# An attention kernel's output projection, by seven block products in place of eight

## The chip, the cores and the metric

The kernel runs on one core of a Trainium2 chip. The metric is the time of one execution on the device in microseconds (us). The kernel before was run three times; a further execution was taken by the hardware profiler, and every profile line below comes from that one.

The engines are named as the profile names them: PE is TensorE's matmuls and PEld its weight loads, DVE is VectorE, ACT is ScalarE, POOL is GpSimd, SP is SyncE, which here only issues transfers. SPq marks rows of SP's queue. L423 is line 423 of the kernel.

## The reference

Sixteen tiles of 128 rows make up x (2048 x 512, bf16). A gate branch B runs beside attention A, and the result is x + A(xn) * silu(B(xn)):

```
xn = layernorm(x)
q  = (xn @ wq) as 32 heads of 128          # k, v: caches, 2048 keys, 32 heads
p  = softmax(q k^T * 128**-0.5)
s  = concat over heads of (p v) @ wo       # wo: 4096 x 512
h  = gelu(layernorm(xn) @ w1), shifted by rows in four column groups
x1 = xn + h @ w2
g  = silu(x1 + gelu(layernorm(x1) @ w3) @ w4)
out = x + s * g
```

## The kernel before

**Units and slots.** The 32 heads are done in eight groups of four (g = 0 to 7; the change's groups two to seven are g = 1 to 6). A unit is one head with one query tile of 512 rows; there are 128, ordered by group, then query tile (qt = 0 to 3), then head (hh = 0 to 3). A unit has eight slots of 256 keys. The main loop (L921 and on) runs over slots n = 8u + p and records every engine's instructions in program order; no scheduler moves them later. In each slot `s_slot` issues two score matmuls of 512 columns into one of two score buffers (`ps_s`) and one exponential of 128x1024 on ScalarE (L423), whose output `pT` is kept for the PV matmuls. These come ten slots later (`pv_slot`, two of 512 columns). The scores of a slot can start only when the exponential two slots earlier has read its buffer.

**Queries.** From unit 16 to 125 the queries of two heads are made together by seven products of 256 columns in place of eight (`product`, `q_take`, `q_part`), in slots 0, 2, 5, 8, 9, 12 and 13 of every sixteen. ScalarE evicts 128x256 twice for it (`q_take`, L393, slots 0 and 5); VectorE does four sums (`q_part`, L400 to L407).

**Softmax sums.** VectorE adds a unit's exponentials up (`add_first` L429, `add_next` L434, `fold` L438, `fold_last` L442). SP transposes the result by a transfer (`turn`, L467, into `tT`); VectorE reduces it (L472) five slots later, takes the reciprocal (L478), and two more transfers through DRAM spread it to all partitions (`dr`, then `rb`). In slot 7 `norm` (L496) multiplies a unit's PV result by it and writes its part of `oT` (128 x 4 heads x 512 rows, two buffers). Its columns come out in an order that the turn gives (row 4r + j next to row j), and the projection picks them with a step of four (`o_cols`).

**Output projection.** Once the four heads of a query tile are normed, `wo_todo` gets its four row tiles t. For each, `wo_mm` accumulates four matmuls of 512 columns (one head each: weights are `oT` columns, the moving operand is `wo_h`) in one PSUM bank (`ps_wo`, tag "xm", one buffer), one row tile per unit, in slots 1, 3, 4 and 6 of even units and 0, 2, 3 and 6 of odd ones (`at_wo`, L965). `wo_post` then adds the bank to `sacc[t]` (fp32, SBUF) on VectorE (L560), in slot 7.

**Gate and end.** `xall` holds the gate tiles. For the query tiles of LATE (2 and 3), `y_scale` and `y_add` multiply `sacc` by the gate and add x before the last groups (L526, L531), and groups 6 and 7 gate their part first (L553) and add it. For the others the last `wo_post` does it (L569 to L572). The last units go another way (from L995 on).

**Queues.** Every transfer of the kernel in attention is issued by SP. GpSimd issues none and is idle from the first 100 us on.

Of the kernel before, what the change touches and what calls it, by code (L numbers as in the profile page):

```python
# [17 lines left out]
def kernel(  # L18
# [25 lines left out]
    NT = Sq // P  # L44
    QT = Sq // 512
# [5 lines left out]
    HG = 4  # L51
# [20 lines left out]
    xall = const.tile([P, NT, D], BF16, name="xall")  # L72
# [21 lines left out]
    drp = ent(pool("drp", 4, bass.MemoryType.DRAM))  # L94
    psO = ent(pool("psO", 2, PSUM))
# [28 lines left out]
    XS = 3 * QT + 1  # L124
    units = [(g, qt, hh) for g in range(NG) for qt in range(QT) for hh in range(HG)]
    LATE = (QT - 2, QT - 1)
    GY = NG - 2
# [61 lines left out]
    xn2T = {}  # L189
    w4_sb = [pR.tile([P, D], BF16, name=f"w4_sb{i}") for i in range(FC)]  # L190
    h2 = {}

# [30 lines left out]
    def ln1_norm(t):  # L223
        if t == 1:
            pin(nc.vector.tensor_scalar(
                out=xall[:, t, :], in0=xin.pop(t)[:], scalar1=less[:], scalar2=rs1[:, t:t + 1],
                op0=ALU.add, op1=ALU.mult))
            return
        src = xin.pop(t)[:]
        w = D // 2 if t == 0 else D  # L230
        for c in range(0, D, w):
            norm_to(xall[:, t, :], src, mv1, rs1, t, slice(c, c + w))

    def tr_pe(t):
        tp = psO.tile([P, DC, P], FP32, tag="ps_o", name="ps_o")
        for dc in range(DC):
            mm(tp[:, dc, :], xall[:, t, dc * P:(dc + 1) * P], ident[:], True, True)
        pin(nc.scalar.activation(out=xnT[:, :, t * P:(t + 1) * P], in_=tp[:], func=ACT.Identity))

    def tr_pe_split(t, parts=((0, 2), (2, 4))):  # L240
        for i in range(2):
            tp = psO.tile([P, 2, P], FP32, tag="ps_o", name="ps_o")
            for j in range(2):
                dc = 2 * i + j
                mm(tp[:, j, :], xall[:, t, dc * P:(dc + 1) * P], ident[:], True, True)
# [6 lines left out]
    def tr_dma(t):  # L252
        pin(nc.sync.dma_start_transpose(out=xnT[:, :, t * P:(t + 1) * P], in_=xall[:, t, :]))
# [21 lines left out]
    def x1(t, ps):  # L275
        pin(nc.vector.tensor_tensor(out=xall[:, t, :], in0=ps[:], in1=xall[:, t, :], op=ALU.add))

    def ln2(t):
# [4 lines left out]
        norm_to(y[:], xall[:, t, :], mv2, rs2, t)  # L283
# [17 lines left out]
    def x2(t, ps):  # L301
        pin(nc.vector.tensor_tensor(out=xall[:, t, :], in0=ps[:], in1=xall[:, t, :], op=ALU.add))

    def gate_tanh(t):
        th = token(False, "th")
        pin(nc.scalar.activation(out=th[:], in_=xall[:, t, :], func=ACT.Tanh, scale=0.5))
        return th

    def gate_silu(t, th):
        pin(nc.vector.scalar_tensor_tensor(  # L310
            out=xall[:, t, :], in0=th[:], scalar=1.0, in1=xall[:, t, :], op0=ALU.add, op1=ALU.mult))
# [11 lines left out]
    def q_copy(u, eng=None):  # L323
        pl, tag = (pR, "qR") if u < HEAD else (qtp, "qT")
        qT = pl.tile([P, 512], BF16, tag=tag, **(dict(bufs=HEAD) if u < HEAD else {}), name="qT")
        if eng is None:
            pin(nc.vector.tensor_copy(out=qT[:], in_=st[u].pop("psq")[:]))
        else:
            pin(nc.scalar.activation(out=qT[:], in_=st[u].pop("psq")[:], func=ACT.Identity))
        st[u]["qT"] = qT  # L330
# [51 lines left out]

    def q_take(v, i):
# [768 lines left out]
```

## Time and profile before

| | us |
|---|---|
| runs, median of 3 (lowest, highest) | 1236.2 (1235.44, 1236.68) |
| the profiled execution | 1236.51 |
| its span, first to last instruction | 1234.7 |
| PE busy | 1228.3 |
| ACT busy | 1105.8 |
| DVE busy | 1030.3 |
| POOL busy | 26.7 |

The page gives for each group of instructions its line, engine, operation and tiles (output <- inputs), the shapes, the count, the busy time and mean duration of one in ns, and the idle time before them with what ended it. The time-ordered view gives the start in us, the duration in us of all instructions merged into the row (xN of them), engine, line, operation and tiles; a bracket at the end is the idle time ahead of it and what ended that. Instructions of one engine overlap in their records, so that a row's duration is not the distance to the next: that is read from the starts or ends of successive rows. Busy shares are unions of such records.

### The profile page before, as it was taken

Reading aid. Unit: us, or ns where it says so; the run is one execution under the profiler, and the core shown is the slowest. Engines: PE = TensorE matmul, PEld = TensorE weight load, DVE = VectorE, ACT = ScalarE, POOL = GpSimd, SP = SyncE. Lnnn points to the kernel's source line nnn. Section 1 sums busy time; section 2 is a strip of 40 time slices with the busy share of each in tenths; the row PEclk is TensorE's granted clock in tenths of the full one; section 3 lists DMA queues with packets and bytes.
Section 4 is the critical chain, followed back from the end, with each engine's and each line's share of the span. In section 5 each row is a group of like instructions: output and inputs, shape, how many; then the busy total and the mean of one; then the engine's idle time right before and its main releaser. Section 6 shows DMA issues by size and latency. Waiting matters only on the chain.

```text
span 1234.7 us, 17537 instructions
## 1 busy us (share of the span) xinstructions
PE 1228.3 (99%) x6267; PEld 644.5 (52%) x6267; DVE 1030.3 (83%) x1647; ACT 1105.8 (90%) x1237; POOL 26.7 (2%) x75
## 2 busy tenths in 40 slices
PE   9999999999999999999999999999999999999998
PEld 6444444455555555555555555555555555555555
DVE  7712778899888888988889888888889999999997
ACT  6345998899999999999999999999999999999996
POOL 5300000000000000000000000000000000000000
PEclk9999999999999999999999999999999999999999
DMA  7761122564344433454244523553346535553342
GB/s 176 171 139 32 29 41 65 95 99 94 57 85 99 104 60 81 88 111 81 62 86 100 111 50 76 102 103 75 74 86 108 105 63 86 103 104 69 77 80 67
DMA packets 244056, 107.75 MB, mean 87 GB/s; under 512 B 194816, under 2 KB 227712, under 8 KB 243968
## 3 DMA queue, kind: packets, MB, share of 16 engines
q1 hardware_dynamic: 243408, 106.17, 42.8%
q8 instruction: 49, 0.80, 0.3%
q14 instruction: 39, 0.32, 0.1%
q10 hardware_dynamic: 560, 0.46, 0.1%
HBM read 67.50 MB, written 2.36 MB: 57 GB/s over the span
## 4 chain that ended last, share of the span: by engine, by line
PE 94%; DVE 3%; DMA 2%; ACT 1%; issue 0%; POOL 0%; DVEq 0%; ACTq 0%
PE ps_s L112 39%; PE ps_o L112 37%; PE ps_wo L112 8%; PE ps_q L112 8%; PE ps_m L112 2%; DVE acc L434 1%; DMA tT<-acc 1%; ACT pT L423 1%; DMA rb<-dr 0%; DVE sm L472 0%; DVE oT L496 0%; DMA xin<-in_A_x_dram 0%; DMA dr<-rc 0%; PE ps_oh L112 0%; DVE acc L438 0%
## 5 line engine op out<-in xcount | busy, mean ns | idle before, releaser
L423 ACT ACTIVATE pT<-ps_s 128x1024 bf16<-128x1024 f32 x1016 | 1016.3, 1025 | 56.6 <-PE ps_s L112 25.9
L112 PE MATMUL ps_s<-qT,kT 128*128 128x512 bf16 (+1 forms) x2064 | 609.1, 377 | 0.0
L112 PE MATMUL ps_o<-pT,vb 128*128 128x512 bf16 x1984 | 589.9, 379 | 0.0
L434 DVE TENSOR_TENSOR acc<-acc,pT 128x2048 bf16<-128x2048 bf16 x254 | 306.9, 1208 | 55.1 <-ACT pT L423 54.7
L112 PEld LDWEIGHTS <-kT 128*128 128x128 bf16 x2064 | 232.6, 113 | 143.9 <-issue 1.0
L112 PEld LDWEIGHTS <-vb 128*128 128x128 bf16 x1984 | 194.0, 98 | 216.8
L429 DVE TENSOR_TENSOR acc<-pT 128x2048 bf16<-128x2048 bf16 x127 | 155.4, 1223 | 37.7 <-ACT pT L423 35.1
L112 PE MATMUL ps_wo<-wo_h,oT 128*128 128x512 bf16 x496 | 186.2, 379 | 0.0
L438 DVE TENSOR_TENSOR acc<-acc 128x1024 bf16<-128x1024 bf16 x127 | 87.4, 688 | 2.5
L496 DVE TENSOR_TENSOR oT<-ps_o,rb 128x512 bf16<-128x512 f32 x127 | 86.6, 682 | 2.4 <-DMA rb<-dr 2.0
L112 PEld LDWEIGHTS <-oT 128*128 128x128 bf16 x528 | 59.0, 112 | 52.5 <-issue 0.7
L472 DVE TENSOR_REDUCE sm<-tT 128x4 f32<-128x512 bf16 x124 | 83.9, 677 | 2.2 <-DMA tT<-acc 2.0
L112 PEld LDWEIGHTS <-wc 128*128 128x128 bf16 x440 | 43.1, 98 | 53.8 <-issue 2.6
L560 DVE TENSOR_TENSOR sacc<-ps_wo,sacc 128x512 f32<-128x512 f32 x96 | 65.7, 684 | 0.0
L112 PEld LDWEIGHTS <-wq_h 128*128 128x128 bf16 x398 | 38.9, 98 | 46.3
L112 PE MATMUL ps_q<-xnT,wq_h 128*128 128x256 bf16 (+1 forms) x288 | 61.1, 298 | 0.4 <-DVE sacc L548 0.4
L407 DVE TENSOR_TENSOR qT<-ps_q,tq 128x512 bf16<-128x512 f32 x55 | 38.0, 691 | 22.8 <-PE ps_q L112 22.3
L442 DVE TENSOR_TENSOR acc<-acc 128x512 bf16<-128x512 bf16 x127 | 52.9, 417 | 0.5
L293 ACT ACTIVATE h2T<-ps_s 128x1024 bf16<-128x1024 f32 x28 | 28.6, 1023 | 25.9 <-PE ps_s L112 25.9
L112 PEld LDWEIGHTS <-w_sb 128*128 128x128 bf16 x368 | 33.5, 98 | 29.6
L112 PE MATMUL ps_s<-xn2T,w_sb 128*128 128x512 bf16 x224 | 48.8, 379 | 0.0
L112 PE MATMUL ps_q<-xs,wc 128*128 128x256 bf16 x246 | 47.0, 273 | 0.0
(102 smaller groups left out, 586.7 us busy)
## 6 DMA issues: line engine op xcount, KB each, us to landing
rb<-dr SPq DMA_DIRECT2D x127, 256.0 KB, 4.1
vb<-in_A_v_cache_dram SPq DMA_DIRECT2D x62, 256.0 KB, 3.1
wq_h<-in_A_wq_dram SPq DMA_DIRECT2D x32, 128.0 KB, 3.1
wo_h<-in_A_wo_dram SPq DMA_DIRECT2D x32, 128.0 KB, 2.9
w_sb<-in_B_w_dram SPq DMA_DIRECT2D x8, 256.0 KB, 5.0
kT<-in_A_k_cache_dram SPq DMA_TRANSPOSE x128, 2.9
xl<-in_A_x_dram SPq DMA_DIRECT2D x16, 128.0 KB, 3.2
dr<-rc SPq DMA_DIRECT2D x127, 2.0 KB, 1.5
```

Of the source, the lines that this page charges most:

```text
L112: pin(nc.tensor.matmul(out=out, lhsT=lhsT, rhs=rhs, start=start, stop=stop, **kw))
L293: pin(nc.scalar.activation(out=h2[c, f][:], in_=ps[:], func=ACT.Gelu_apprx_tanh))
L407: pin(nc.vector.tensor_tensor(out=s["q"][:, 1:3, :], in0=ps[:], in1=s["u"][:].unsqueeze(1).to_broadcast([P, 2, 256]), op=ALU.add))
L423: pin(nc.scalar.activation(out=s["pT"][-1][:, jj:jj + 2, :], in_=sps[:], func=ACT.Exp, scale=SCALE))
L429: pin(nc.vector.tensor_tensor(out=s["acc"][:], in0=s["pT"][0][:], in1=s["pT"][1][:], op=ALU.add))
L434: pin(nc.vector.tensor_tensor(out=a[:], in0=a[:], in1=st[u]["pT"][i][:], op=ALU.add))
L438: pin(nc.vector.tensor_tensor(out=a[:, 0:2, :], in0=a[:, 0:2, :], in1=a[:, 2:4, :], op=ALU.add))
L442: pin(nc.vector.tensor_tensor(out=a[:, 0, :], in0=a[:, 0, :], in1=a[:, 1, :], op=ALU.add))
L472: pin(nc.vector.tensor_reduce(out=sm[:], in_=s["tT"][:], axis=mybir.AxisListType.X, op=ALU.add))
L496: pin(nc.vector.tensor_tensor(out=to, in0=o, in1=rb, op=ALU.mult))
L560: pin(nc.vector.tensor_tensor(out=sa, in0=ps[:], in1=sa, op=ALU.add))
```

## The change

For groups 1 to 6 (`BLOCK`) the product of `oT` and `wo` is done on 2 x 2 blocks, by seven products in place of eight. The rows of a query tile are halved into two column halves of `oT` (WL, WR: row tiles 0 and 1, and 2 and 3), the inner dimension into head pairs (UP, DOWN), the columns of `wo` into halves of 256. i = 0, 1 names the tile in each half, so a product for one i serves the row tiles i and i + 2, and one (g, qt, i) is a block of sixteen slots. `wo_sum` makes four sums of weight blocks per group, `o_sum` four sums of `oT` blocks per query tile, on VectorE. `wo_product` issues two matmuls of 256 columns for each of the seven products.

Of the five sums that products go into, three are taken by VectorE from PSUM into `sacc` (`wo_take`: 512 columns in slot 13, 256 columns in slot 21, which is slot 5 of the next sixteen). Two are evicted by ScalarE to SBUF (`wo_aside`, fp32, slots 7 and 15, two staging buffers) and added into DRAM (`both`) by transfers that GpSimd issues; group 6's `wo_join` adds them into `sacc` by four more transfers per block.

`sacc` becomes a tile for two row tiles, in column halves. The query columns are turned where queries are evicted (`q_copy`, `q_take`, `q_part` read PSUM with a step of four), so `oT` comes out in row order and is read without a step; the score matmuls then read the paired queries in runs of 64. `xall` is split: tiles 0 to 7 (`xlo`) live only until attention starts, their gates are stored to DRAM by GpSimd (`gate_silu`) and loaded again for group 7 (`fin_load`). `y_add` is gone; `y_scale` lets a transfer add x. Group 6's own gating leaves `wo_post`.

```
+    AWAY = NT // 2
...
+    TW = (2, 1, 0, 1)
...
+        if t < AWAY:
+            gates[t] = keep.tile([P, D], BF16, tag=f"gate{t}", name="gate")
+            pin(nc.gpsimd.dma_start(out=gates[t][:], in_=xg(t)))
...
+        if u in TURN:
+            src = src.rearrange("d (r j) -> d j r", j=4)
+            dst = dst.rearrange("d (j r) -> d j r", j=4)
...
+            for j in range(2):
+                x = q[:, 2 * j:2 * j + 2]
+                st[v + j] = dict(qT=x.rearrange("d h j r -> d j h r"))
+            out = q[:, 0]
+        pin(nc.scalar.activation(out=out, in_=turned(v, s["ps"][:])[:, 0], func=ACT.Identity))
...
+    def wo_sum(g, i):
+        w = wog[g]
+        b11, b12, b21, b22 = (w[:, k, c] for k in (UP, DOWN) for c in (WL, WR))
+        out = b12 if i == 2 else pS.tile([P, 2, D // 2], BF16, tag=f"tw{i}", bufs=TW[i], name="tw")[:]
+        a, b = ((b12, b11), (b22, tw.get((g, 0))), (b22, b12), (b21, tw.get((g, 1))))[i]
+        pin(nc.vector.tensor_tensor(out=out, in0=a, in1=b, op=ALU.subtract))
...
+    def o_sum(g, qt, i):
+        o = oTs[(g, qt)]
+        a11, a12, a21, a22 = (o[:, k, c] for c in (WL, WR) for k in (UP, DOWN))
+        out = pS.tile([P, 2, D // 2], BF16, tag=f"so{i}", bufs=1, name="so")
+        a, b, op = ((a21, a22, ALU.add), (so.get(0), a11, ALU.subtract),
+                    (a11, a21, ALU.subtract), (a12, so.get(1), ALU.subtract))[i]
+        pin(nc.vector.tensor_tensor(out=out[:], in0=a, in1=b, op=op))
...
+    def wo_product(g, qt, i, k):
+        if k == 1:
+            wo_ps[0] = psX.tile([P, 2, D // 2], FP32, tag="xm", name="ps_wo")
...
+        side, a, b = {
+            1: (0, a11, b11),
+            2: (0, a12, b21),
+            3: (1, so.get(3), b22),
+            4: (1, a22, tw.get((g, 3))),
+            5: (1, so.get(0), tw.get((g, 0))),
+            6: (0, so.get(1), tw.get((g, 1))),
+            7: (1, so.get(2), tw.get((g, 2))),
+        }[k]
+        for j in range(2):
+            mm(wo_ps[0][:, side, :], a[:, j, i * P:(i + 1) * P], b[:, j, :],
+               k in (1, 6) and j == 0, True, skip_group_check=True)
+
+    def wo_aside(g, qt, i):
+        stage = pS.tile([P, 2, D // 2], FP32, tag="tm", bufs=2, name="stage")
+        pin(nc.scalar.activation(out=stage[:], in_=wo_ps[0][:], func=ACT.Identity))
+        kw = dict(accum_op=ALU.add)
+        if (qt, i) not in shared:
+            shared[qt, i] = keep.tile([P, 2, D // 2], FP32, tag=f"both{qt}{i}", name="both")
+            kw = {}
+        pin(nc.gpsimd.dma_start(out=shared[qt, i][:], in_=stage[:], **kw))
+
+    def wo_take(g, qt, i, last):
+        sa, ps = sp[qt, i], wo_ps[0]
+        cols = slice(2, 3) if last else slice(0, 2)
+        pin(nc.vector.tensor_tensor(
+            out=sa[:, cols], in0=ps[:, 1:2] if last else ps[:], in1=sa[:, cols], op=ALU.add))
+
+    def wo_join(qt, i):
+        sa, both = sp[qt, i], shared.pop((qt, i))
+        for j in (1, 2, 3):
+            pin(nc.gpsimd.dma_start(out=sa[:, j], in_=both[:, 0], accum_op=ALU.add))
+        pin(nc.gpsimd.dma_start(out=sa[:, 3], in_=both[:, 1], accum_op=ALU.add))
...
-        if (g * QT + qt) * HG + hh in TURN:
-            return o.rearrange("k (p j) -> k j p", j=4)[:, ts, :]
...
+        pin(nc.gpsimd.dma_start(out=sacc[t], in_=halves(xsrc[t]), accum_op=ALU.add))
-
-    def y_add(t):
-        xl = fin.pop(t)
-        pin(nc.vector.tensor_tensor(out=sacc[t][:], in0=sacc[t][:], in1=xl[:], op=ALU.add))
...
+    for g in BLOCK:
+        for qt in range(QT):
+            u0 = ((g * QT + qt) * HG + 6) * SPU
+            if qt == 0:
+                for i, n in ((0, -19), (2, -11), (1, -1), (3, 3)):
+                    o_at(u0 + n, wo_sum, g, i)
+            for i, n in ((2, 5), (0, 7), (1, 11), (3, 15)):
+                o_at(u0 + n, o_sum, g, qt, i)
+            for i in range(2):
+                a = u0 + 16 * i
+                for k, n in ((1, 6), (7, 7), (2, 10), (4, 11), (6, 14), (5, 15), (3, 17)):
+                    steps[a + n].append((wo_product, g, qt, i, k))
+                for n in (7, 15):
+                    steps[a + n].append((wo_aside, g, qt, i))
+                o_at(a + 13, wo_take, g, qt, i, False)
+                o_at(a + (21 if g < BLOCK[-1] or qt < QT - 1 or i == 0 else 18), wo_take, g, qt, i, True)
+                if g == BLOCK[-1]:
+                    o_at(a + 22, wo_join, qt, i)
+                    if qt in LATE:
+                        for j in range(2):
+                            at(a + 42 + 5 * j, lambda t=4 * qt + i + 2 * j: y_scale(t))
...
         run_steps(n, product)
+        run_steps(n, wo_product)
+        run_steps(n, wo_aside)
         run_steps(n, q_take)
...
+        if u // HG == (NG - 1) * QT + 1 and u % HG in (2, 3):
+            at_wo = ([4, 5, 6, 7], [2, 3, 5, 6, 7])[u % 2]
```

155 lines of the change are left out of this document (90 added, 65 removed).

## The prediction

> **What bounds the kernel now.** First the page's busy shares and its chain of waits, then the busy time by stretches.
>
> ```profile
> PE 1228.3 (99%) x6267; PEld 644.5 (52%) x6267; DVE 1030.3 (83%) x1647; ACT 1105.8 (90%) x1237; POOL 26.7 (2%) x75
> PE 94%; DVE 3%; DMA 2%; ACT 1%; issue 0%; POOL 0%; DVEq 0%; ACTq 0%
> 100.00:150.00 50.00, 50.00 (x233) 23.50 (x232) 24.02 (x32) 37.58 (x41) 0.00 (x0) 1.00 0.07 11
> 550.00:650.00 100.00, 100.00 (x505) 52.76 (x504) 85.62 (x131) 95.70 (x107) 0.00 (x0) 1.00 0.40 82
> ```
>
> In a stretch the columns are sum, PE, PEld, DVE, ACT, POOL, granted clock, share of the DMA engines, GB/s. Through attention TensorE never rests, at full clock. ScalarE is next at 95.7%, so whatever it gets in addition has to be followed place by place. The time-ordered view of one pair of units shows the rhythm:
>
> ```profile
> 69.81 12.25 PE L112 MATMUL ps_o<-w_sb,h2T 128*128 128x512 bf16 x56
> ...
> 605.36 0.59 PE L112 MATMUL ps_s<-qT,kT 128*128 128x512 bf16 x2
> 605.79 0.59 PE L112 MATMUL ps_o<-pT,vb 128*128 128x512 bf16 x2
> 606.22 0.38 PE L112 MATMUL ps_q<-xnT,wq_h 128*128 128x256 bf16 x2
> 606.44 0.59 PE L112 MATMUL ps_s<-qT,kT 128*128 128x512 bf16 x2
> ...
> 615.08 0.59 PE L112 MATMUL ps_s<-qT,kT 128*128 128x512 bf16 x2
> ```
>
> The 56 matmuls of the first row follow each other at (12.25 - 0.38)/55 = 0.2158 us. A slot is two score and two PV matmuls, 4 x 0.2158 = 0.863 us, plus what is put behind them: here a pair of 256-column query products; one 512-column projection matmul elsewhere. ScalarE's rows for the same two units:
>
> ```profile
> 615.71 8.42 ACT L423 ACTIVATE pT<-ps_s 128x1024 bf16<-128x1024 f32 x8 [0.21 <-PE ps_s L112]
> 624.02 0.39 ACT L393 ACTIVATE tq<-ps_q 128x256 f32<-128x256 f32 x1
> 624.28 5.20 ACT L423 ACTIVATE pT<-ps_s 128x1024 bf16<-128x1024 f32 x5
> 629.38 0.38 ACT L393 ACTIVATE qT<-ps_q 128x256 bf16<-128x256 f32 x1
> 629.64 2.92 ACT L423 ACTIVATE pT<-ps_s 128x1024 bf16<-128x1024 f32 x3
> 632.78 1.02 ACT L423 ACTIVATE pT<-ps_s 128x1024 bf16<-128x1024 f32 x1 [0.21 <-PE ps_s L112]
> ```
>
> The pattern repeats after 632.78 - 615.71 = 17.07 us, sixteen slots. TensorE does 64 + 8 matmuls of 512 columns and 14 of 256 in it: 72 x 0.2158 = 15.54, so the fourteen take 1.53 us, 0.1094 each.
>
> **TensorE's part of the change.** In groups 1 to 6 every sixteen slots have eight 512-column projection matmuls (1.726 us), afterwards seven pairs of 256 columns: 14 x 0.1094 = 1.532. That is 0.194 us less for each of 6 groups x 4 query tiles x 2 = 48 blocks, **-9.3 us**. Their positions (slots 1, 6, 7, 10, 11, 14, 15 of sixteen) miss those of the query products (0, 2, 5, 8, 9, 12, 13), so fourteen slots last 0.863 + 0.219 = 1.082 us and slots 3 and 4 last 0.863.
>
> **ScalarE's part.** Each block adds two evictions of 128x512 (`wo_aside`), in slots 7 and 15. Their price comes from these rows and the ones above:
>
> ```profile
> 229.16 4.69 ACT L423 ACTIVATE pT<-ps_s 128x1024 bf16<-128x1024 f32 x5 [0.21 <-PE ps_s L112]
> ...
> 221.36 1.94 ACT L423 ACTIVATE pT<-ps_s 128x1024 bf16<-128x1024 f32 x2
> ...
> 222.86 0.59 PE L112 MATMUL ps_o<-pT,vb 128*128 128x512 bf16 x2
> 223.35 0.59 PE L112 MATMUL ps_s<-qT,kT 128*128 128x512 bf16 x2
> ...
> L329 ACT ACTIVATE qT<-ps_q 128x512 bf16<-128x512 f32 x12 | 7.2, 597 | 5.7 <-PE ps_q L112 5.7
> ```
>
> Five exponentials without a rest end (4.69 - 1.02)/4 = 0.917 us apart. A query eviction of 256 ends 0.28 us after the exponential before it (624.02 + 0.39 against 615.71 + 8.42). The line between the two gives 0.49 us for 512. Its bounds are 0.28 (the 256 row) and 0.60 (the whole 597 ns of the 512 row, were nothing overlapped). In sum ScalarE needs 16 x 0.917 + 2 x 0.28 + 2 x 0.49 = 16.2 of 16.9 us: it fits, but not everywhere. An exponential can start 0.63 us after its scores do (615.08 to 615.71); the scores two slots on need its buffer, and go 0.05 us after it ends (221.36 + 1.94 = 223.30, next scores 223.35, where 222.86 + 0.43 was possible: TensorE already waits for ScalarE there, with no extra work in the slots). From the scores of slot 15 on, ScalarE does: 0.63, exponential 1.02, eviction 0.49, exponential of slot 0 0.92, query eviction 0.28, three exponentials 2.75; together 6.09, and 0.05 to the scores of slot 5. TensorE is there after four slots of 1.082 and two of 0.863 = 6.05. It waits **0.09 us in every block, +4.3 us in 48**. With 0.28 for the eviction the wait is gone, with 0.60 it is 0.20 and the whole gain with it. From slot 7 the same sum leaves some 0.05 us to spare at slot 10.
>
> [...]
>
> The query evictions and sums now read the score buffer's columns with a step of four. VectorE's `norm` reads PSUM in steps already and takes no longer than an unstepped read of its size:
>
> ```profile
> 613.59 0.68 DVE L560 TENSOR_TENSOR sacc<-ps_wo,sacc 128x512 f32<-128x512 f32 x1
> 614.19 0.68 DVE L496 TENSOR_TENSOR oT<-ps_o,rb 128x512 bf16<-128x512 f32 x1
> ```
>
> For ScalarE no row has it: between nothing and double (0.21 us for 256 elements, which slot 0's place in the sum above hands on in full, +10 us). I take nothing, by VectorE's rows.
>
> **VectorE's part.** Per block one 128x512 and one 128x256 addition replace two 128x512; two sums of head pairs are added, four weight sums per group.
>
> ```profile
> 609.53 0.41 DVE L442 TENSOR_TENSOR acc<-acc 128x512 bf16<-128x512 bf16 x1
> 610.29 1.22 DVE L429 TENSOR_TENSOR acc<-pT 128x2048 bf16<-128x2048 bf16 x1 [0.34 <-ACT pT L423]
> 612.45 1.23 DVE L434 TENSOR_TENSOR acc<-acc,pT 128x2048 bf16<-128x2048 bf16 x1 [0.94 <-ACT pT L423]
> ...
> 614.79 0.68 DVE L472 TENSOR_REDUCE sm<-tT 128x4 f32<-128x512 bf16 x1
> ...
> 617.64 0.42 DVE L405 TENSOR_TENSOR qT<-ps_q,tq 128x256 bf16<-128x256 f32 x1
> ```
>
> 96 + 24 operations of L442's size at 0.41 add 49 us, 48 additions shrink from 0.68 to 0.42 (-12 us), and the last groups lose 16 operations of 0.68 (-11): +26 us on 1030, some 85%. The additions move from behind slot 7 to slot 5, into the 0.94 us in which L434 waits for an exponential: 0.42 + 0.41 fit. The next product into the same PSUM bank (slot 6) leaves 6 x 1.08 + 0.86 after 605.36, at 612.70; the addition that it waits for ends near 610.29 + 1.22 + 0.42 = 611.93. Cover 0.8 us; **0 us**. Without it each 0.1 us costs 48 x 0.1 = 4.8 us.
>
> **DMA and the rest.** GpSimd's queue gets transfers, most of which add to their destination; no row has one. Per block 2 x 256 KB go into DRAM; group 6 adds 32 of 128 KB back into SBUF and 8 of x; 8 gate tiles are stored before attention.
>
> ```profile
> q1 hardware_dynamic: 243408, 106.17, 42.8%
> rb<-dr SPq DMA_DIRECT2D x70, 256.0 KB, 4.1
> tT<-acc SPq DMA_TRANSPOSE x70, 3.7
> ```
>
> A transfer of 256 KB lands in 4.1 us. Nobody waits for an adding one before the next into the same place (8 slots, 8.5 us) and the eviction that needs its staging buffer (two later, 16.9 us): even at double, 8.2 us, it is **0**. Only past 16 us would ScalarE stall. 42.8% of 16 engines x 1234.7 us for 106 MB is 80 engine-us per MB, so a block's 0.52 MB adds 15% to the engines' load, or 31% if what is added to is read as well. The gates go out where the engines are all but idle (7% in 100 to 150 us) and come back a unit early; the joins are issued from unit 104 to 119 and their sums are first read in units 117 to 121. SP's queue changes by two entries.
>
> ```profile
> PE ps_q L112 <- DVE qT L405: 1.1, 3, 0.6
> ```
>
> These waits fall in the stretch where the old kernel gates and adds x with extra VectorE operations. Half of those leave: **-0.5 us**, bounds 0 and -1.1.
>
> **Sum.** -9.3 + 4.3 - 0.5 = -5.5. The profiled execution took 1236.5 (span 1234.7 and 1.8 around it), 0.3 above the median of the runs; so 1231.0 for such an execution and **1230.7** for the median.
>
> **Rivals.** *Everything hidden.* ScalarE keeps up in every slot (eviction nearer its lower bound): 1236.2 - 9.3 - 1.1 = 1226. For it: no wait of this kind in the dense stretches now. Against: the 0.05 us already lost in 223.35.
>
> *ScalarE longer than counted.* Eviction 0.60: 1236; stepped reads doubled instead: 1241; both: 1246. For it: neither has a row.
>
> *Transposes land late (slower).* The adding transfers raise the engines' load from 43% to 58 or 74%. The place is `tT`:
>
> ```profile
> 609.98 1.20 SPq L467 DMA_TRANSPOSE tT<-acc  x1
> 952.26 5.14 DMA tT<-acc
> 959.44 0.60 DVE sacc L526
> ```
>
> Issued at 609.98, landed 3.7 later at 613.7, read at 614.79: 1.1 us to spare, some 0.7 when VectorE runs earlier as above. L405 ends at 618.06 and the product behind it leaves in slot 12, 615.08 + 3 x 1.08 + 0.86 = 619.18: 1.1 more. Past 3.7 + 0.7 + 1.1 = 5.5 us each microsecond is one per block. At 952.26 one landing of 5.14 together with L526 in its way gave the 0.6 us wait above. With 6.0 us as the rule: +24 us, 1255. Against: 3.7 is the median at 43% load, and a landing would have to take half as long again in nearly every block.
>
> *Narrow matmuls cost more than half.*
>
> ```profile
> L112 PEld LDWEIGHTS <-kT 128*128 128x128 bf16 x1124 | 126.7, 113 | 71.9 <-issue 0.2
> L112 PEld LDWEIGHTS <-wq_h 128*128 128x128 bf16 x212 | 20.7, 98 | 25.0
> ```
>
> Were a weight load (98 ns) not hidden behind a 256-column matmul, 14 x 0.207 against 1.726 would cost 1.17 us per block, 1287 us. The query products with their own 98 ns loads already run at 0.109, which speaks against it. [...]
>
> *Reading the turned queries in runs of 64 slows the score matmuls.* Stepped weights (kT) load in 113 ns against 98; 15 ns on 1,728 score matmuls is +26 us, 1257. The load's own delay is hidden, so this is only the nearest row.
>
> **How the numbers follow.** Forecast 0.46 (own range 1228 to 1233.7); everything hidden 0.14; ScalarE longer 0.20, of it 0.12 within 0.2% (2.5 us, about what runs of this kernel can tell from no change) and 0.08 slower; transposes late 0.15; narrow matmuls 0.02; runs of 64 0.03. Faster 0.60, same 0.12, slower 0.28. The range 1225.5 to 1247 takes in both bounds of the eviction and of the stepped reads and leaves out the last three cases for the most part, some 0.18.
>
> **What would show it.** Right: projection pairs 0.109 apart; a period of 16.96 us; short waits of score matmuls for L423's successor once per sixteen slots, before slot 5; evictions ending 0.49 after an exponential; `tT` landing under 5.5 us; VectorE near 85%. Wrong: a period of 16.87 (all hidden) or over 17.07; waits of projection matmuls for VectorE; waits of VectorE for `tT`; of ScalarE for a transfer; score matmuls more than 0.216 apart.

## The result, and the profile after

| | us |
|---|---|
| runs before, median of 4 (lowest, highest) | 1236.18 (1235.44, 1236.68) |
| runs after, median of 4 (lowest, highest) | 1295.15 (1285.8, 1296.21) |
| ratio | 1.0461, interval 1.0438 to 1.0485 |
| the profiled execution after, and its span | 1285.8, 1283.7 |

The change makes the kernel 4.6% slower. 1230.7 was forecast and the range ended at 1247. The page of the kernel after, its busy shares, the chain of waits, two groups, two queues:

```profile
PE 1237.0 (96%) x6555; PEld 663.3 (52%) x6555; DVE 1047.3 (82%) x1751; ACT 1127.9 (88%) x1333; POOL 147.8 (12%) x219
...
q1 hardware_dynamic: 243408, 106.17, 40.9%
q0 software_dynamic: 20480, 32.52, 19.8%
...
PE 42%; DMA 31%; DVE 20%; ACT 3%; issue 2%; SPq 2%; DVEq 0%; ACTq 0%
PE ps_s L114 18%; PE ps_o L114 15%; DMA rb<-dr 13%; DMA dr<-rc 13%; DMA tT<-acc 5%; DVE acc L458 4%; DVE sm L496 3%; PE ps_q L114 3%; DVE oT L520 3%; PE ps_wo L114 3%; ACT pT L447 3%; PE ps_m L114 2%; DVE acc L453 2%; SPq L146 1%; DVE so L5
...
L520 DVE TENSOR_TENSOR oT<-ps_o,rb 128x512 bf16<-128x512 f32 x127 | 87.5, 689 | 87.3 <-DMA rb<-dr 86.7
```

Before, the chain that ended last was TensorE's own work to 94%. Now TensorE holds 42% of it and transfers 31%, and two of them lead the list: `dr`, the store of a unit's reciprocals into DRAM, and `rb`, the load that spreads them. `norm` (now L520) waits 86.7 us in all for that load; before it waited 2.0 us:

```profile
L496 DVE TENSOR_TENSOR oT<-ps_o,rb 128x512 bf16<-128x512 f32 x127 | 86.6, 682 | 2.4 <-DMA rb<-dr 2.0
```

The profiled execution is the fastest of the four after, some 9 us under the other three. The busy time by stretches shows where TensorE rests:

```profile
450.00:550.00 100.00, 100.00 (x545) 55.72 (x543) 91.48 (x153) 98.59 (x118) 9.37 (x11) 1.00 0.70 111
550.00:650.00 100.00, 96.03 (x517) 52.60 (x515) 86.02 (x142) 93.95 (x112) 9.71 (x12) 1.00 0.67 109
1050.00:1150.00 100.00, 85.78 (x450) 45.85 (x449) 73.88 (x125) 83.34 (x100) 26.16 (x30) 1.00 0.83 129
350.00:1250.00 900.00, 858.26 (x4550) 466.42 (x4549) 772.20 (x1277) 833.47 (x988) 114.39 (x133) 1.00 0.69 116
```

From 350 to 1250 us it rests 900 - 858.3 = 41.7 us: up to 4.3 us in each 100 us up to 1050, none from 450 to 550, and most where the joins of group 6 run (1050 to 1150 us). The granted clock is 1.00 in these rows. What the transfers of 400 to 1000 us took, first before, then after (KB each, median us from issue to landing; the other rows of before stand in the prediction):

```profile
dr<-rc SPq DMA_DIRECT2D x70, 2.0 KB, 1.5
```

```profile
both<-stage POOLq DMA_DIRECT2D x68, 256.0 KB, 4.8
rb<-dr SPq DMA_DIRECT2D x68, 256.0 KB, 3.6
...
tT<-acc SPq DMA_TRANSPOSE x69, 3.8
dr<-rc SPq DMA_DIRECT2D x68, 2.0 KB, 3.3
```

The load `rb` lands sooner (3.6 us, 4.1 before), the turn `tT` about as it did (3.8, 3.7 before), and the loads of keys and values take 3.5 us in place of 3.0. The transfer that takes more than twice as long is the smallest: 2 KB in 1.5 us before, 3.3 now. In these 600 us there are 68 units of 8.8 us where 70 of 8.5 stood before. One of them in the time-ordered view of the kernel after, on VectorE, then on SP, then on GpSimd:

```profile
708.59 0.69 DVE L520 TENSOR_TENSOR oT<-ps_o,rb 128x512 bf16<-128x512 f32 x1 [1.23 <-DMA rb<-dr]
709.20 0.42 DVE L562 TENSOR_TENSOR so<-oT 128x512 bf16<-128x512 bf16 x1
709.53 0.68 DVE L496 TENSOR_REDUCE sm<-tT 128x4 f32<-128x512 bf16 x1
710.24 0.18 DVE L502 RECIPROCAL rc<-sm 128x4 f32<-128x4 f32 x1
```

```profile
701.95 0.32 SPq L504 DMA_DIRECT2D dr<-rc  x1
705.30 0.32 SPq L508 DMA_DIRECT2D rb<-dr  x1
705.67 1.22 SPq L491 DMA_TRANSPOSE tT<-acc  x1
...
709.59 1.17 SPq L162 DMA_DIRECT2D vb<-in_A_v_cache_dram  x1
710.86 0.52 SPq L504 DMA_DIRECT2D dr<-rc  x1
```

```profile
700.52 0.85 POOL L591 DMA_DIRECT2D both<-stage  x1 [7.72 <-ACT stage L586]
```

GpSimd issues its adding transfer 1.4 us ahead of the small store; it lands at 705.00, the store at 705.28. SP holds the load until the store has landed, 705.30 - 701.95 = 3.35 us later; the load lands 3.29 later and `norm` starts at 708.59. The next unit's reduce stands behind `norm` on VectorE, with one of the new sums (L562) between them: 0.94 us to its start, 0.71 to the reciprocal, 0.62 to the next store, which also waits for SP to have issued a load of values. That is a ring from store to store: 3.35 + 3.29 + 0.94 + 0.71 + 0.62 = 8.91 us, where TensorE needs 16.96/2 = 8.48. SP's queue carries the delay on: the turn stands behind the load, goes out 3.72 us after the store and lands at 709.43, only 0.1 us before the reduce that reads it starts.

The same ring before, on SP:

```profile
607.47 0.33 SPq L480 DMA_DIRECT2D dr<-rc  x1
608.87 0.33 SPq L484 DMA_DIRECT2D rb<-dr  x1
...
615.71 0.33 SPq L480 DMA_DIRECT2D dr<-rc  x1
```

1.40 for the store, 4.1 for the load, 615.71 - 614.19 = 1.52 from `norm` to the next store: 7.0 us in a unit of 8.53. **The ring had a cover of 1.5 us, and the prediction did not look at it.**

The stretch from 450 to 550 us, in which TensorE never rests, shows what matters. The adding transfers run there too, but ten of its twelve small stores land ahead of the adding transfer nearest to them, and all ten go out just before it or at most 0.54 us behind its start. One such unit, on GpSimd, then on SP:

```profile
500.23 0.84 POOL L591 DMA_DIRECT2D both<-stage  x1 [7.53 <-ACT stage L586]
```

```profile
500.36 0.32 SPq L504 DMA_DIRECT2D dr<-rc  x1
501.76 0.32 SPq L508 DMA_DIRECT2D rb<-dr  x1
```

This store takes 1.4 us. From 350 to 1050 us 51 stores go out later than the 0.85 us that GpSimd takes to issue the adding transfer ahead: none lands before that transfer, 28 land within 0.4 us behind it. Of the 25 that go out sooner 18 land ahead of it.

### The profile page after: what moved, and what is told of

Read it like the earlier page. It is cut to its first block, busy times and chain, and to the rows that moved or that the text cites. A ratio compares the mean times of both kernels' runs of the same rounds, so it can differ in the third digit from the quotient of the medians.

```text
span 1283.7 us, 18666 instructions
## 1 busy us (share of the span) xinstructions
PE 1237.0 (96%) x6555; PEld 663.3 (52%) x6555; DVE 1047.3 (82%) x1751; ACT 1127.9 (88%) x1333; POOL 147.8 (12%) x219
## 4 chain that ended last, share of the span: by engine, by line
PE 42%; DMA 31%; DVE 20%; ACT 3%; issue 2%; SPq 2%; DVEq 0%; ACTq 0%
PE ps_s L114 18%; PE ps_o L114 15%; DMA rb<-dr 13%; DMA dr<-rc 13%; DMA tT<-acc 5%; DVE acc L458 4%; DVE sm L496 3%; PE ps_q L114 3%; DVE oT L520 3%; PE ps_wo L114 3%; ACT pT L447 3%; PE ps_m L114 2%; DVE acc L453 2%; SPq L146 1%; DVE so L562 1%
## 5 line engine op out<-in xcount | busy, mean ns | idle before, releaser
L447 ACT ACTIVATE pT<-ps_s 128x1024 bf16<-128x1024 f32 x1016 | 1008.9, 1050 | 83.1 <-PE ps_s L114 66.3
L591 POOL DMA_DIRECT2D both<-stage x96 | 82.2, 856 | 898.7 <-ACT stage L586 858.3
L520 DVE TENSOR_TENSOR oT<-ps_o,rb 128x512 bf16<-128x512 f32 x127 | 87.5, 689 | 87.3 <-DMA rb<-dr 86.7
L496 DVE TENSOR_REDUCE sm<-tT 128x4 f32<-128x512 bf16 x124 | 84.3, 680 | 19.6 <-DMA tT<-acc 19.3
L462 DVE TENSOR_TENSOR acc<-acc 128x1024 bf16<-128x1024 bf16 x127 | 87.4, 688 | 2.5
L114 PE MATMUL ps_wo<-wo_h,oT 128*128 128x256 bf16 (+1 forms) x304 | 77.3, 312 | 4.0 <-DVE sacc L596 4.0
L114 PEld LDWEIGHTS <-oT 128*128 128x128 bf16 x432 | 41.9, 98 | 51.9 <-issue 7.4
L114 PEld LDWEIGHTS <-so 128*128 128x128 bf16 x384 | 37.0, 98 | 54.4 <-issue 8.1
L586 ACT ACTIVATE stage<-ps_wo 128x512 f32<-128x512 f32 x96 | 59.7, 622 | 0.0
L114 PE MATMUL ps_q<-xnT,wc 128*128 128x256 bf16 x194 | 37.0, 272 | 22.7 <-DVE qT L429 22.4
L596 DVE TENSOR_TENSOR sacc<-ps_wo,sacc 128x512 f32<-128x512 f32 x96 | 52.9, 551 | 0.0
```

Source lines behind the costliest of these rows:

```text
L114: pin(nc.tensor.matmul(out=out, lhsT=lhsT, rhs=rhs, start=start, stop=stop, **kw))
L447: pin(nc.scalar.activation(out=s["pT"][-1][:, jj:jj + 2, :], in_=sps[:], func=ACT.Exp, scale=SCALE))
L462: pin(nc.vector.tensor_tensor(out=a[:, 0:2, :], in0=a[:, 0:2, :], in1=a[:, 2:4, :], op=ALU.add))
L496: pin(nc.vector.tensor_reduce(out=sm[:], in_=s["tT"][:], axis=mybir.AxisListType.X, op=ALU.add))
L520: pin(nc.vector.tensor_tensor(out=to, in0=o, in1=rb, op=ALU.mult))
L586: pin(nc.scalar.activation(out=stage[:], in_=wo_ps[0][:], func=ACT.Identity))
```

## The experiments

Runs that were taken together share a chip (r1 to r4; r12, r7, r8, r10; r6, r9, r11, r13; r14, r16, r17, r18; r19, r20), and each ratio is to runs of the kernel before on it; the second and the third of these groups ran on one chip. What the transfers cost differs from chip to chip: the change is at 1.0461 in the runs above and at 1.0597 in r12, while the kernel before stays at 1236 to 1237 us on all of them.

### Taking the transfers away, part by part

**r1**: no transfers from `wo_aside` and no joins; evictions, products and sums stay.

```
     def wo_aside(g, qt, i):
         stage = pS.tile([P, 2, D // 2], FP32, tag="tm", bufs=2, name="stage")
         pin(nc.scalar.activation(out=stage[:], in_=wo_ps[0][:], func=ACT.Identity))
-        kw = dict(accum_op=ALU.add)
...
-        pin(nc.gpsimd.dma_start(out=shared[qt, i][:], in_=stage[:], **kw))
...
-                    o_at(a + 22, wo_join, qt, i)
```

> The changed kernel without the transfers of the evicted sums (neither into DRAM nor back; ScalarE's evictions stay; the output lacks these two of the five sums). Theory 'loop': a unit of groups 1 to 6 takes what the loop dr, rb, norm, reduce, reciprocal, dr takes (8.8 us in 400 to 1000 us), because an adding transfer in flight holds up dr from 1.5 to 3.3 us. Then dr is back at 1.5 us, VectorE's waits for rb are gone and the time is the forecast's, 1228 to 1234. Rival 'evictions': ScalarE's two evictions per block hold TensorE up; then it stays above 1270.

Measured 1235.54 us, 0.9988 of before (0.9977 to 1.0000). The transfers are the whole loss against the kernel before; a gain clear of the noise is not left either. The store lands in 1.6 us:

```profile
dr<-rc SPq DMA_DIRECT2D x71, 2.0 KB, 1.6
```

With nothing else in the way the same run tests ScalarE's step. Its matmuls in order of time:

```profile
609.02 0.59 PE L114 MATMUL ps_o<-pT,vb 128*128 128x512 bf16 x2
609.49 0.59 PE L114 MATMUL ps_s<-qT,kT 128*128 128x512 bf16 x2
609.92 0.59 PE L114 MATMUL ps_o<-pT,vb 128*128 128x512 bf16 x2
610.40 0.59 PE L114 MATMUL ps_s<-qT,kT 128*128 128x512 bf16 x2
...
612.35 0.38 PE L114 MATMUL ps_wo<-wo_h,oT 128*128 128x256 bf16 x2
612.56 0.60 PE L114 MATMUL ps_s<-qT,kT 128*128 128x512 bf16 x2
...
626.44 0.59 PE L114 MATMUL ps_s<-qT,kT 128*128 128x512 bf16 x2
```

The period is 626.44 - 609.49 = 16.95 us (16.96 forecast). Two matmuls of 512 take 0.43, but the scores at 609.49 and 610.40 come 0.47 and 0.48 after the ones ahead: two waits of together 0.09 us, the price that was worked out, in two places in place of one.

**r2**: plain transfers in place of adding ones (the last block written stands; the joins stay).

```
-        pin(nc.gpsimd.dma_start(out=shared[qt, i][:], in_=stage[:], **kw))
+        pin(nc.gpsimd.dma_start(out=shared[qt, i][:], in_=stage[:]))
```

> The changed kernel with every transfer into DRAM a plain store in place of an adding one (the two sums then hold only the last block's part). If what delays dr is that the destination is read and added, dr falls to about 2 us and the time below 1255. If it is any 256 KB in the engines at that time, dr stays near 3 us and the time at 1275 or more.

1257.14 us, 1.0159 (1.0116 to 1.0202), between the two. The transfer lands in 2.9 us in place of 4.8, and the small store beside it still takes 2.6, so a plain transfer delays it too. But a store of 2.6 us nearly fits under the cover: from 350 to 1050 us TensorE rests 3.5 us, where the change rests 18.9. Most of what is left of the loss lies from 1050 to 1250 us (15.4 us of rest, 22.8 in the change), where the joins and the additions of x still add.

**r3**: adding transfers as in the change, no joins.

```
-                    o_at(a + 22, wo_join, qt, i)
```

> The changed kernel without group 6's 32 transfers back into SBUF (the output lacks the two sums). Loop: the stretch from 1050 us on, where a unit takes 10 us in place of 8.8, loses its 1.2 us for about 20 units: 1258 to 1272. Rival: that stretch is slow through the x additions and the gated end, not the joins: above 1280.

1302.29 us, 1.0524 (1.0493 to 1.0555). TensorE is busy 95.5% from 1050 to 1150 us where the change has 85.8%, which would put the joins at some 10 us there; but `norm` waits 121 us for `rb` in all, where the change waits 87, and the end of the run is no earlier. A miss as an experiment on the total: the changed kernel didn't run beside it.

**r4**: `norm` moved behind the next unit's reduce on VectorE, to open the ring there.

```
         if p == 0 and 1 <= u:
             if u - 2 in TURN:
                 turned_sums(u - 2)
                 turned_recip(u - 2)
+            if u - 3 in TURN:
+                norm(u - 3)
...
-        if p == norm_p and u - 2 in TURN:
-            norm_queue(u - 2)
```

> The changed kernel with norm moved in VectorE's order from slot 7 behind the next unit's reduce and reciprocal (slot 0); all transfers stay. Loop: the reduce no longer stands behind a wait for rb, so dr leaves earlier and the loop is open; dr stays at about 3.3 us, but VectorE's waits for rb fall from 87 us to under 20, units in 400 to 1000 us take 8.5 in place of 8.8 us, and the time is 1245 to 1270. Rival 'load': the DMA engines' load makes everything late wherever VectorE waits; then it stays above 1280.

1303.82 us, 1.0536 (1.0506 to 1.0567): the expectation failed. Its waits, from 300 to 1250 us:

```profile
DVE sm L496 <- DMA tT<-acc: 117.2, 75, 5.2
...
PE ps_o L114 <- DVE oT L520: 56.1, 44, 4.1
```

The waits for `rb` are gone and waits for the turn stand in their place. The ring closes a second time on SP: the load waits there for the store, the turn stands behind the load, and the reduce needs the turn before the next store can go. Opening one of two orders moves the wait; no gain is seen (1.0536 here, 1.0461 and 1.0597 for the change, which did not run beside it).

### The ring, opened; the transfers alone

**r12** is the change itself, for reference.

> The changed kernel itself, beside the others on one chip: 1285 to 1302 us, the small stores 3.3 us each in the stretch 400 to 1000 us. It is the reference for the edits that run with it; no theory hangs on it.

1310.07 us, 1.0597 (1.0565 to 1.0630), longer than expected. Its profile has no stretch like the one from 450 to 550 us above: from 350 to 1050 us TensorE is busy at most 96.4% of any 100 us, the store takes 3.6 us, and none lands before the adding transfer ahead of it.

**r7**: as r4, and the turn ahead of the load on SP.

```
-        if p == 1 and u - 2 in TURN:
-            bcast(u - 2)
...
         if p == 3 and u - 1 in TURN:
             turn(u - 1)
+        if p == 3 and u - 2 in TURN:
+            bcast(u - 2)
```

> Both links of the loop opened at once: the scaling stands behind the next unit's reduce on VectorE, and the turning transfer is issued ahead of the broadcast load on SP, so that the turn waits for no small store. Theory (a loop of small store, broadcast load and scaling, closed once by VectorE's order and once by SP's): with both open nothing goes round, the turn is in time, TensorE loses under 3 us from 350 to 1000 us, and what is left is the end of group six with its joining transfers, some 12 to 18 us: 1248 to 1258 us. Rival (the adding transfers load the engines, and whatever is due late waits): the waits go to another place as they did with the scaling moved alone, and the time stays at 1285 to 1305 us.

1270.83 us, 1.0274 (1.0254 to 1.0294): 39 us less than the change beside it, where r4 alone showed no gain. It falls short of the 1258 expected. The store still takes 3.2 us, the load now goes out 4.9 us after it, behind the turn, and lands at 9.0; `norm` then holds up TensorE's next PV bank (26.2 us in all from 300 to 1250 us).

**r8**: the adding transfer is held back until the next unit's last fold, by a small GpSimd copy that reads its result.

```
+    def aside_go(u):
+        while asides:
+            to, stage, kw = asides.pop(0)
+            pin(nc.gpsimd.tensor_copy(out=junk[:], in_=st[u]["acc"][:, 0, 0:1]))
+            pin(nc.gpsimd.dma_start(out=to[:], in_=stage[:], **kw))
...
+                aside_go(u - 1)
```

> The adding transfer is issued after the last fold of the next unit, some 3 us later, so that it is not in flight when the small store goes out; bytes and number of transfers are the same. Theory (the small store is what the adding transfer delays): the store lands in 1.5 to 2.0 us again, store to broadcast landed in at most 6.3 us, TensorE loses under 10 us from 350 to 1050 us, 1250 to 1268 us with the joins of group six. Rival (load of the engines): broadcast and turn take the delay in place of the store (broadcast load over 5 us or turn over 5 us), 1285 to 1300 us.

1280.03 us, 1.0354 (1.0298 to 1.0411), 30 us less than the change beside it, between the two expectations. Its transfers from 400 to 1000 us:

```profile
tT<-acc SPq DMA_TRANSPOSE x68, 4.8
dr<-rc SPq DMA_DIRECT2D x67, 2.0 KB, 1.9
```

Both theories are half right: the store is nearly free again, and the turn, which now starts with the adding transfer, pays a microsecond in its place (4.8 us, 3.8 in the change).

**r10**: the kernel before, with one adding transfer of 256 KB from GpSimd in each of 96 units, out of an `sacc` tile into DRAM.

```
+    def extra_add(u):
+        pin(nc.gpsimd.tensor_copy(out=junk[:], in_=st[u]["pT"][-1][:, 2, 0:1]))
+        k, kw = (u // HG % QT, u % 2), dict(accum_op=ALU.add)
...
+        pin(nc.gpsimd.dma_start(out=shared[k][:], in_=sacc[4 * ((u // HG + 2) % QT) + u % HG][:], **kw))
...
+        if p == 7 and 22 <= u < 118:
+            extra_add(u)
```

> The kernel before with one adding transfer of 256 KB from GpSimd in each of 96 units, issued after the unit's last exponential; it computes what it did, and the sums in DRAM go nowhere. No block products, no evictions, no joins. Theory (the transfers alone make the loop): small stores of 3.0 to 3.5 us, store to broadcast landed 6.6 to 7.0 us, a unit of 8.65 to 8.85 us in place of 8.53, so 1246 to 1268 us, with VectorE's scaling waiting for the broadcast in most units. Rival (it takes the change's own order of VectorE and ScalarE to make the transfers matter): the stores are as late, but the scaling has the time: 1236 to 1240 us.

1279.05 us, 1.0342 (1.0318 to 1.0366): 42 us, more than expected, with none of the change's products, evictions and joins. Its transfers and the first wait of VectorE, from 400 to 1000 us:

```profile
both<-sacc POOLq DMA_DIRECT2D x67, 256.0 KB, 4.9
rb<-dr SPq DMA_DIRECT2D x66, 256.0 KB, 3.5
...
tT<-acc SPq DMA_TRANSPOSE x67, 3.8
dr<-rc SPq DMA_DIRECT2D x67, 2.0 KB, 3.6
```

```profile
DVE oT L498 <- DMA rb<-dr: 65.6, 55, 2.5
```

The same picture in a kernel that is otherwise the one before. In the mean over 400 to 1000 us its unit takes 9.0 us from store to store: 3.5 until the load goes out, 3.7 for the load, 1.8 from `norm` to the next store. The last was 1.5 in the kernel before; here the reduce in it also waits for the turn, which lands within 0.15 us of it in 62 of 67 units. So the ring is closed at both its places, VectorE and SP, and (9.0 - 8.53) x 96 = 45 us is near the 42 measured.

### The other steps, and the size of the transfer

**r6**: r1 without ScalarE's evictions.

```
-        stage = pS.tile([P, 2, D // 2], FP32, tag="tm", bufs=2, name="stage")
-        pin(nc.scalar.activation(out=stage[:], in_=wo_ps[0][:], func=ACT.Identity))
+        pass
```

> The run without transfers, and without ScalarE's two evictions per block as well; left out is the part of the sums that two of the five accumulations would have carried. Theory (the evictions make TensorE wait 0.09 us per block before the scores of slots four and five): 48 blocks by 0.087 us = 4.2 us less than the run without transfers, so 0.9945 to 0.9960 of before, 1230.5 to 1232.5 us. Rival (those waits are only moved to the next engine in line): 0.9985 as without transfers.

1231.99 us, 0.9949 (0.9935 to 0.9963); r1, on another chip, had 0.9988. The difference of 0.0039 is 4.8 us, by the medians 3.6; 4.3 was forecast for ScalarE. The length of a period shows it directly. Two score pairs sixteen slots apart:

```profile
600.60 0.59 PE L114 MATMUL ps_s<-qT,kT 128*128 128x512 bf16 x2
...
617.47 0.59 PE L114 MATMUL ps_s<-qT,kT 128*128 128x512 bf16 x2
```

617.47 - 600.60 = 16.87 us, where r1 has 16.95 and the kernel before 17.07: the products are worth 0.20 us per block, the evictions take 0.08 of it back.

**r9**: r1 without the additions of x.

```
-        pin(nc.gpsimd.dma_start(out=sacc[t], in_=halves(xsrc[t]), accum_op=ALU.add))
```

> The run without transfers, and without the additions of x by DMA near the end as well, so that GpSimd issues no transfer after the first stage; x is left out of eight output tiles. Theory (the 4 to 6 us that the run without transfers loses between 1100 and 1200 us come from these additions, by the same small stores): dr back to 1.6 us in that stretch, 1229.5 to 1231.5 us, 0.994 to 0.996 of before. Rival (VectorE's order near the end, or the group changes, lose them): 1234.5 to 1236 us.

1233.40 us, 0.9968 (0.9957 to 0.9980), against 0.9988 for r1: eight adding transfers of 128 KB would cost some 2 us, half of what was expected. r1 ran on another chip and the two intervals overlap, so it is not shown that they cost anything.

**r11**: GpSimd adds the two sums itself, from the staging tile into `sacc`; no transfer, no joins.

```
+        sa = sp[qt, i]
+        for j in (1, 2, 3):
+            pin(nc.gpsimd.tensor_tensor(out=sa[:, j], in0=stage[:, 0], in1=sa[:, j], op=ALU.add))
+        pin(nc.gpsimd.tensor_tensor(out=sa[:, 3], in0=stage[:, 1], in1=sa[:, 3], op=ALU.add))
```

> The two sums that went by DMA into DRAM are added by GpSimd out of the staging tile straight into the accumulators, four additions of 128x256 for each block (two blocks in 17 us); no transfer into DRAM and no joins. Theory (only the transfers hurt): as without transfers, 1233 to 1238 us, 0.997 to 1.001 of before. Rival (GpSimd's additions get in VectorE's way): VectorE's mean times longer and TensorE waiting, 1242 to 1265 us.

1265.70 us, 1.0232 (1.0217 to 1.0246): the rival. VectorE's groups by form from 400 to 1000 us, first of r1, then of r11:

```profile
L462 DVE TENSOR_TENSOR acc<-acc 128x1024 bf16<-128x1024 bf16 x71 | 48.8, 687 | 1.2
L520 DVE TENSOR_TENSOR oT<-ps_o,rb 128x512 bf16<-128x512 f32 x71 | 48.7, 685 | 5.1 <-DMA rb<-dr 4.6
```

```profile
L462 DVE TENSOR_TENSOR acc<-acc 128x1024 bf16<-128x1024 bf16 x68 | 66.5, 978 | 1.2
L520 DVE TENSOR_TENSOR oT<-ps_o,rb 128x512 bf16<-128x512 f32 x68 | 46.2, 680 | 5.8 <-DMA rb<-dr 5.6
```

The fold L462, with both inputs in SBUF, takes 978 ns in place of 687; `norm` (L520), which reads PSUM, takes 680 in place of 685.

**r13**: r10 with half the bytes (128 KB each).

```
-            shared[k] = keep.tile([P, 512], FP32, tag=f"both{k[0]}{k[1]}", name="both")
+            shared[k] = keep.tile([P, 256], FP32, tag=f"both{k[0]}{k[1]}", name="both")
```

> The kernel before with the same 96 adding transfers at half the bytes (128 KB each). Theory (the small store stands behind the bytes of the adding transfer, so its delay goes with them): the store takes 2.3 to 2.8 us, the loop comes out under the unit of 8.53 us in most units, 1240 to 1255 us. Rival (any adding transfer delays the store by a fixed time): the store at 3.3 to 3.6 us and 1270 to 1280 us as with the whole bytes.

1244.16 us, 1.0054 (1.0038 to 1.0070). The time is the theory's, the store is not: it takes 3.0 us, nearer the 3.6 of whole bytes than the 1.5 of none. In the mean over 400 to 1000 us a unit takes 8.6 us here and 9.0 in r10, 8.54 in the kernel before: the first 1.2 us by which the store is later fall nearly all into the cover, and the next half a microsecond lengthens the unit by 0.4. That is why it is worth 35 us.

### The store taken out, and what helps together

**r14**: from unit 20 on every broadcast load reads one and the same tile, so there is no store in the ring.

```
+        if u < 20 or "one" not in kept:
...
+            pin(nc.sync.dma_start(out=s["dr"][:], in_=rc[:]))
+        else:
+            s["dr"] = kept["one"]
```

> The changed kernel with one small store in all from unit 20 on: the broadcast loads read that one tile, so they wait neither for a store nor for the reduce (the scaling factors are those of one unit; left out is each unit's own). Adding transfers, evictions, joins, orders of VectorE and SP as in the change. Theory (the delayed small store is what closes the loop): TensorE loses under 8 us from 350 to 1050 us and the scaling waits for hardly any load; the joins of group six stay, so 1245 to 1262 us. Rival (the load on the engines makes broadcast and turn late by themselves): 1280 to 1305 us, with the scaling still waiting for the load or the reduce for the turn.

1236.43 us, 1.0005 (0.9995 to 1.0014): all 96 adding transfers, 32 joins and 8 additions of x are still there, and the whole loss is gone. Waits for `rb` come to 1.5 us in all, for `tT` to 1.4. A stretch of it, and its transfers from 400 to 1000 us:

```profile
550.00:650.00 100.00, 99.47 (x534) 55.76 (x543) 90.79 (x150) 98.72 (x119) 10.22 (x12) 1.00 0.57 112
```

```profile
rb<-dr SPq DMA_DIRECT2D x72, 256.0 KB, 3.5
both<-stage POOLq DMA_DIRECT2D x71, 256.0 KB, 4.0
...
tT<-acc SPq DMA_TRANSPOSE x71, 2.5
```

Load on the engines alone (0.57 of them busy in this stretch, 0.40 in the kernel before) therefore costs nothing here. The edit removes more than the store's delay, though: the load no longer waits for the reduce either, and SP never stands. Which share the delay has by itself isn't told by it; the stretch from 450 to 550 us of the change, where the store gets ahead of the adding transfer and all else stays, speaks for most.

**r18**: r10 with both orders opened as in r7.

> The kernel before with the 96 adding transfers of 256 KB, and both links opened as in the changed kernel: scaling behind the next reduce, turn ahead of the broadcast load. Theory (a loop of store, load, scaling and reduce sets the unit): the small stores stay at 3 to 3.6 us and the time falls from 1279 to 1240 to 1256 us. Rival (late transfers cost wherever they stand): 1268 to 1285 us.

1261.16 us, 1.0202 (1.0187 to 1.0218), against 1.0342 for r10 on another chip. By that part of the loss goes, less than expected, the same as in r7.

**r16**: r7 without the joins. **r17**: r7 with the two sums staged and kept as bf16, half the bytes.

```
-        stage = pS.tile([P, 2, D // 2], FP32, tag="tm", bufs=2, name="stage")
+        stage = pS.tile([P, 2 * D], BF16, tag="tm", bufs=2, name="stage")[:, 0:D].rearrange("p (a c) -> p a c", a=2)
```

> The run with both links opened, and without the joining transfers of group six (left out is the adding of the two shared sums). Theory (joins cost on their own, by load in one group): 10 to 18 us less than with them, 1253 to 1261 us; what is left over before is the long way from small store to landed broadcast, 9.0 us. Rival (the joins only took the place of other waits, as when they were left out of the change): 1267 to 1273 us.

> Both links opened, and the two shared sums staged and kept in DRAM as bf16: half the bytes in the adding transfers and in what the joins read. Theory (the cost goes with the bytes and with the loop): half the bytes cost 7 us in the kernel before where whole bytes cost 42, so here most of the 34 us that are left go: 1238 to 1252 us. Rival (the number of adding transfers is what costs): 1262 to 1272 us.

r16: 1244.12 us, 1.0069 (1.0052 to 1.0085). r17: 1245.12 us, 1.0074 (1.0059 to 1.0089). Both gain more on r7 than expected. r7 ran on other chips (1.0274, and 1.0282 below), and r16 is quicker than r7 in stretches without joins too (99.3% busy against 95.3% from 950 to 1050 us), so the joins' own price stays open.

**r19**: r17 with r8's later transfer. **r20**: r7 again, beside it.

> Everything that helped, together: both links opened, the two shared sums as bf16 in DRAM, and the adding transfer issued after the next unit's last fold, clear of the small store. Theory (what is lost is the way from small store to scaling): the store lands in under 2 us, TensorE loses little outside group six, 1234 to 1243 us. Rival (the later transfer now delays the turn, which the reduce awaits): 1243 to 1260 us.

> The run with both links opened, again, on one chip with the run above, since the chips so far differ in what the adding transfers cost (the change was at 1295 and 1310 us): 1255 to 1275 us. If the bytes and the moment of the transfer matter, it is over 10 us longer than the run above; if not, within 5 us.

r19: 1260.20 us, 1.0186 (1.0169 to 1.0203). r20: 1271.86 us, 1.0282 (1.0258 to 1.0305). Bytes and moment are worth 12 us on one chip, but r19 is a miss: the store still takes 2.6 us, in half of the units with no adding transfer in flight. In this order of SP the load of one unit is still landing, with loads of keys and values, when the next unit's store goes out.

No version with its transfers and its sums whole came out ahead of the kernel before. The best that left only sums out is r6, 5 to 6 us ahead.

## Why the prediction was wrong

- **TensorE, -9.3 us: right.** In r1 a pair of projection matmuls stands between PV and scores for 612.56 - 612.35 = 0.21 us (0.219 taken), and the period has the forecast length to 0.01 us. Without the evictions it is 16.87 us (r6), 0.20 under the kernel before (0.194 taken).
- **ScalarE, +4.3 us: right.** 0.09 us per block seen in r1, and gone in r6; 3.6 to 4.8 us won there by leaving the evictions out.
- **VectorE, 0: right by itself.** In the whole of r1 projection matmuls and their weight loads wait 0.7 us for VectorE's additions and 1.4 us for its new sums. The sums counted there came back elsewhere: the 0.33 us of L562 between `norm` and reduce lie in the ring.
- **-0.5 us from fewer waits for the query sums: wrong in sign, small.** r1 has 4.7 us of such waits in place of 1.1, 1.8 us without the additions of x (r9).
- **DMA, "0": the step that failed.** Its numbers held: an adding transfer landed in 4.8 us (4.1 to 8.2 given), the engines' load rose from 43 to 61% (58 to 74 given), only GpSimd's own joins waited for an adding transfer, and `tT` landed in 3.8 us, far under the 5.5 at which the rival was to decide. VectorE still waited 19.3 us for `tT` in all (2.0 before), because the turn went out late behind the load. But the sentence asked who waits for the new transfer, not which old one it delays, and the rival's place was chosen by the turn, which had 1.8 us of room by the prediction's own sum. The ring of store, load, `norm` and reduce had 1.5 us, and its first link, whose time the prediction quoted nowhere, went from 1.5 to 3.3 us. So the term that was put at 0 made nearly all of the 55 us by which the profiled execution missed its forecast (1285.8 against 1231.0). How near the threshold lies is shown by r13 and r10: a store 1.5 us late costs 7 us, one 2.1 us late 42.
- **The rival "transposes land late"** was right in kind, a transfer past its cover, and wrong in place. Its price, the excess times the number of blocks, is right in kind too: (8.8 - 8.48) x 96 = 31 us. Most of the other 24 us falls behind 1050 us, where TensorE rests 22.8 us up to 1250 and joins and additions of x run beside the ring; what they do there is not shown.
- **The forecast without the transfers**, 1230.7 against 1236.2, is 0.9956. r9, where GpSimd issues nothing in attention, has 0.9968 (0.9957 to 0.9980): all other steps together were some 1.5 us off, with x left out in eight tiles.

What stays open: how much of the loss is the store's delay alone and how much SP standing behind it, what the joins cost by themselves, and why the chips differ.

## What to carry to other kernels

A transfer that nobody waits for is not free (96 of them cost 42 us in r10): cost what it delays, and begin with the smallest transfers on a path that goes round from unit to unit. For each such ring add up its links once round, across every queue in which one link stands behind another, and compare with the period; the difference is the cover, and a delay was here nearly free up to it and paid in every unit beyond it (7 us in all for a store 1.5 us late, 42 for one 2.1 us late). If a ring closes in two orders (an engine's and a queue's), opening one may only move the wait, as in r4, where 117.2 us of waits for the turn took the place of those for the load.

## What the runs showed of the hardware

The store of 2 KB goes out as 128 pieces of 16 bytes. Its median landing by what else was in flight, worked out from the transfers' issue and landing times between 350 and 1050 us (a transfer counts when both are under way together for over 0.3 us; rarer mixes are not listed):

```
before:  nothing          1.40 us (41 stores)   a load of values  1.72 (20)   keys and values  2.05 (7)
after:   adding transfer  2.81 us (32)          with values       3.57 (14)   with keys and values  3.51 (15)
r10:     adding transfer  3.58 us (29)
r13:     half the bytes   2.99 us (32)
```

r10 and r13 differ in the bytes alone, and their rows by 0.6 us. The store's landing goes with that of the adding transfer: in r10 77 of 78 stores land after the one ahead of them and 41 of these 0.1 to 0.4 us after it, in r13 78 of 82 and 55. In this stretch the adding transfer lands in 4.8 us in r10 and 3.7 in r13, but in r13 the store goes out sooner behind it, 0.9 us in place of 1.7, so that half the bytes shorten the store by less than the transfer. It looks like waiting for the transfer ahead, not like a share of bandwidth; the cause is not shown, as no run here looks inside an engine.

An adding transfer of 256 KB from GpSimd landed in 4.8 us, a plain one from the same queue in 2.9 (r2).

GpSimd's additions out of SBUF (r11) came with a longer fold of two SBUF inputs on VectorE (L462: 978 ns, 687 in r1), while `norm` (L520), which reads PSUM, took 680 ns (685 in r1).
